# Top-k attention with a highway feed-forward layer on one core: joined remainder groups, fewer check operations, another order at the start and at the end

## The chip, the cores and the metric

The kernel runs on one core of a Trainium2 chip. The metric is the device time of one execution in microseconds (us). The kernel before was timed three times: 926.5, 925.96 and 923.73, median 925.96. The profile is of one more execution, of 925.72.

## The reference

Eight batches of eight heads, 576 rows, head dimension 64. For each row of scores only the 32 largest count, the softmax is taken over these, and the result, laid side by side for the eight heads, goes through a highway layer of width 512.

```python
scores = scale * np.matmul(q, k.transpose(0, 1, 3, 2))
kth = np.partition(scores, -top_k, axis=-1)[..., -top_k:-top_k + 1]
scores = np.where(scores >= kth, scores, -1000000000.0)
attn = softmax(scores);  x = attn @ v, heads side by side
H = np.maximum(x @ w_h, 0.0);  T = sigmoid(x @ w_t + b_t)
out = T * H + (1.0 - T) * x
```

## The kernel before

**Tiles and steps.** A batch has 576 = 4 x 128 + 64 rows, hence five groups: four of 128 rows and a remainder of 64. A full group has eight tiles (one a head), handled two at a time as "pairs", four pairs; in a remainder group two heads share a tile of 128 partitions, so there are four tiles and two pairs. That makes 18 pairs a batch and 144 in all, in 40 groups. The main loop has one step n for each pair and some more to drain. In step n, work on several pairs is interleaved: the score matmuls of pair n+1 (`scores`, into a four-bank tile `ps` of which there is one) and their evacuation by ScalarE into z (`evac`); the first reduction of pair n on VectorE (`tree`, the operation hi<-ps,z); for two pairs together the next two halvings (`folds`) and the minima that belong to them, on GpSimd (POOL; `minima`, with integer arithmetic); the first half of the top-k lists of two pairs (`tops`), in even steps, and the rest (`rest`) in odd steps, all MAX8 and MATCH_REPLACE8 on VectorE, which leaves the 32nd largest in m4; the penalty of pair n-4 (`mask`, ScalarE); transposes of scores and penalty with an exponential on the way out (`trans`); the product with v of pair n-5 (`av`) and its copy to xs.

**End of a group.** `norm` takes the reciprocal of the sums (VectorE) and multiplies (POOL) to x. The feed-forward layer follows in three pieces, one a step, from a list: `ffn_x` (transposes xtps, copies xT and xh on ScalarE), `ffn_h` and `ffn_d` (matmuls hps on TensorE, then d on VectorE), `ffn_t`, `ffn_e` and `ffn_o` (matmuls tps, tanh on ScalarE, d again on VectorE, o on POOL, store by SyncE). All of xtps, hps, tps and kqps use the pool `fps`, which has one bank: the next cannot begin until the last is read.

**Loads.** For each pair of heads `prep_pair` loads k, q and v (four loads each: two heads, main part and end), transposes k and q on TensorE into kqps and copies them out on ScalarE. The first batch does it in the first four steps, ahead of `tree`; later batches spread it. All loads and stores but a few are issued by SyncE (SP) in one queue. The weights are loaded from POOL's queue in step 1.

**Checks.** After each group `settle` (POOL, three operations: room, slack, reach) records how far the lists reached; at the end VectorE reduces these records, TensorE transposes the result, and a flag says whether a second, exact body has to run. It is read by all engines into a register, and a branch follows.

**What sets the order.** All instructions of TensorE, VectorE, ScalarE and POOL in the main body are recorded in program order (`Pinned`, L35, so that nearly all rows carry this line). SyncE's order is chosen by the scheduler.

The order of a step in the kernel before, and its drain:

```python
while step < NPR + 6 or ffn:
    ...
    if have(n):
        ops.tree(n)
    ...
    if have(n - 4):
        ops.mask(n - 4, *pairs[n - 4], tis=(0,))
    ...
    if have(n - 5):
        ops.av(n - 5, g, pi, preps[g.b][2])
    if have(n - 4):
        ops.mask(n - 4, *pairs[n - 4], tis=(1,))
```

Of the kernel before, what the change touches and what calls it, by code (L numbers as in the profile page):

```python
# [18 lines left out]
WIDE = 600.0  # L19
J = 4  # L20
# [26 lines left out]
class Group:  # L47


    def __init__(self, b, qt, gi, H, P):  # L50
        self.b, self.qt, self.gi = b, qt, gi
        self.rem = qt == J
        self.qlen = P // 2 if self.rem else P
        tiles = (
            [(2 * hp, 2 * hp + 1) for hp in range(H // 2)]
            if self.rem
            else [(h,) for h in range(H)]
        )
        self.nt = len(tiles)
        self.pairs = [tiles[i : i + 2] for i in range(0, self.nt, 2)]  # L60


class Ops:
# [31 lines left out]
    def load_pair(self, src, hp, name, eng=None):  # L95
        nc, D, S, R, P = self.nc, self.D, self.S, self.R, self.P
        JP = J * P
        t = self.ldpool.tile([P, J + 1, 2, D], FP32, tag=name, name=name)
        eng = eng or nc.sync
        for hh in range(2):  # L100
            h = 2 * hp + hh
            eng.dma_start(
                t[:, 0:J, hh, :], src(h, 0, JP).rearrange("(p j) d -> p j d", j=J)
            )
            eng.dma_start(t[0:R, J, hh, :], src(h, JP, S))
        return t
# [6 lines left out]
    def prep_pair(self, srcs, hp, prep, qeng=None):  # L113

        nc, D, S, R, P = self.nc, self.D, self.S, self.R, self.P
        JP = J * P
        kT, qT, vb = prep
        ins = {}

        def load():  # L120
            ins["k"] = self.load_pair(srcs[1], hp, "kin")
            ins["q"] = self.load_pair(srcs[0], hp, "qin", qeng)
            ins["v"] = self.load_pair(srcs[2], hp, "vin")

        def main(name, dst):
            kqps = self.fps.tile([P, 512], FP32, tag="fp", name="kqps")
            for c in range(J):
                nc.tensor.transpose(
                    kqps[:, c * P : (c + 1) * P],
                    ins[name][:, c, :, :].rearrange("p h d -> p (h d)"),  # L130
                    self.ident[:],
                )
            nc.scalar.copy(dst[:, hp, 0:JP], kqps[:])

        def last():
            kqps = self.fps.tile([P, 512], FP32, tag="fp", name="kqps")
            for i, name in enumerate("kq"):
                nc.tensor.transpose(
                    kqps[:, i * R : (i + 1) * R],
                    ins[name][0:R, J, :, :].rearrange("p h d -> p (h d)"),  # L140
                    self.ident[0:R, 0:R],
                )
            for i, dst in enumerate((kT, qT)):
                nc.scalar.copy(dst[:, hp, JP:S], kqps[:, i * R : (i + 1) * R])

        def values():
            vdst = vb[:, 2 * hp : 2 * hp + 2, :, 0:D].rearrange("p h c d -> p c h d")
            nc.scalar.copy(vdst[:, 0:J], ins["v"][:, 0:J])
            nc.scalar.copy(vdst[0:R, J], ins["v"][0:R, J])

        return [load, lambda: main("k", kT), lambda: main("q", qT), last, values]


# [47 lines left out]
    def folds(self, k, g, pi):  # L201
# [4 lines left out]
        if pi == 0:  # L206
            g.w2 = self.lpool.tile([P, H, H2 + 24], FP32, tag="w2", name="w2")
# [29 lines left out]
    def tops(self, g, t, h3, hl):  # L237
# [5 lines left out]
        m1, m2, w2 = g.m1[:, t, :], g.m2[:, t, :], g.w2[:, t, :]  # L243
# [13 lines left out]
    def rest(self, g, t, lo):  # L257
# [6 lines left out]
        w2 = g.w2[:, t, :]  # L264
# [29 lines left out]
    def lists(self, n, g, pi):  # L294
        P, H = self.P, self.H
        if pi == 0:
            for name in ("m1", "m4") if self.exact else ("m1", "m2", "m4"):
# [20 lines left out]
    def settle(self, g):  # L318
# [7 lines left out]
            self.room[:, g.gi, 0:nt, 0:3],  # L326
            thr.unsqueeze(2).to_broadcast([P, nt, 3]),
# [3 lines left out]
        gp.tensor_tensor(  # L331
            self.slack[:, g.gi, 0:nt, 0], g.m2[:, 0:nt, 7], thr, ALU.subtract
        )
        gp.tensor_copy(self.reach[:, g.gi, 0:nt], g.m1[:, 0:nt, 0])
# [44 lines left out]
    def trans(self, n):  # L379
# [4 lines left out]
        zr = self.zrps.tile([P, 512], FP32, tag="zr", name="zr")  # L384
        for ti in range(2):
            self.chunk_T(zr[:, ti * P : (ti + 1) * P], z, pen, ti, J)
        nc.scalar.activation(
            et[:, :, J, :],
            zr[:, 0 : 2 * P].rearrange("p (t j) -> p t j", t=2),
            AF.Exp,  # L390
            scale=self.scale,
        )
# [10 lines left out]
        self.st[n].update(et=et, zr=zr)  # L403

    def av(self, n, g, pi, vb):
# [4 lines left out]
        if pi == 0:  # L410
            g.xs = self.xpool.tile([P, self.H * DE], FP32, tag="xs", name="xs")
        ql = g.qlen
        c0 = col = 0 if g.rem else 2 * P
        h0 = g.pairs[pi][0][0]
        for ti, heads in enumerate(g.pairs[pi]):
            for hi, h in enumerate(heads):
                q0 = hi * (P // 2)
                for c in range(J + 1):
                    nc.tensor.matmul(
                        zr[0:ql, col : col + DE],  # L420
# [6 lines left out]
        nc.scalar.copy(g.xs[0:ql, h0 * DE : h0 * DE + col - c0], zr[0:ql, c0:col])  # L427
# [3 lines left out]
    def norm(self, g):  # L431
        nc, P, H, D = self.nc, self.P, self.H, self.D
        ql = g.qlen
        xs3 = g.xs[0:ql, :].rearrange("p (h e) -> p h e", e=D + 1)
        rinv = self.xpool.tile([P, H], FP32, tag="rinv", name="rinv")
        nc.vector.reciprocal(rinv[0:ql, :], xs3[:, :, D])
        g.x = self.xpool.tile([P, H * D], FP32, tag="x", name="x")
        nc.gpsimd.tensor_tensor(
# [6 lines left out]
    def ffn_x(self, g):  # L445
        nc, P, n_g, ql = self.nc, self.P, self.n_g, g.qlen
# [16 lines left out]
    def ffn_h(self, g):  # L463
        nc, P, n_g, ql = self.nc, self.P, self.n_g, g.qlen
# [10 lines left out]
    def ffn_d(self, g):  # L475

        ql = g.qlen
# [10 lines left out]
    def ffn_t(self, g):  # L488

        nc, P, n_g, ql = self.nc, self.P, self.n_g, g.qlen  # L490
        g.ps = self.fps.tile([P, 512], FP32, tag="fp", name="tps")
# [13 lines left out]
    def ffn_e(self, g):  # L505

        ql = g.qlen
# [9 lines left out]
    def ffn_o(self, g, dst):  # L517
        ql = g.qlen
        o = self.fpool.tile([self.P, self.dm], FP32, tag="o", name="o")
        self.nc.gpsimd.tensor_tensor(o[0:ql, :], g.x[0:ql, :], g.d[0:ql, :], ALU.add)  # L520
        self.nc.sync.dma_start(dst, o[0:ql, :])
# [3 lines left out]
def kernel(  # L525
# [17 lines left out]
    assert D == 64 and R == 64 and H % 4 == 0 and dm == 512  # L543
# [13 lines left out]
    nc.vector.tensor_scalar_mul(nident[:], ident[:], -STEEP)  # L557
# [11 lines left out]
    for i in range(2):  # L569
# [5 lines left out]
    room = const([P, NG, H, 3], FP32, "room")  # L575
    nc.gpsimd.memset(room[:], 1.0)
    slack = const([P, NG, H, 1], FP32, "slack")
    nc.gpsimd.memset(slack[:], 1.0)
    reach = const([P, NG, H], FP32, "reach")
    nc.gpsimd.memset(reach[:], 1.0)  # L580
# [8 lines left out]
        room=room, slack=slack, reach=reach,  # L589
    )  # L590

    with ExitStack() as cm:
# [12 lines left out]
        def srcs(b):  # L605
            return [
                (lambda h, r0, r1, t=t: t[b, h, r0:r1, :]) for t in (q, k, v)
            ]

        def out_rows(g):  # L610
            if not g.rem:
                r0 = g.b * S + g.qt
                return out[r0 : r0 + JP : J, :]
            r0 = g.b * S + JP
            return out[r0 : r0 + R, :]

        groups = [
            Group(b, qt, b * nck + qt, H, P) for b in range(B) for qt in range(nck)
        ]
        pairs = [(g, pi) for g in groups for pi in range(len(g.pairs))]  # L620
# [6 lines left out]
        def prep(b, hp, qeng=None):  # L627
            if hp == 0:
                preps[b] = ops.prep_alloc(vbufs[b % 2])
            return ops.prep_pair(srcs(b), hp, preps[b], qeng)  # L630
# [20 lines left out]
        early = [prep(0, hp, nc.scalar if hp == 0 else None) for hp in range(NHP)]  # L651
# [8 lines left out]
        step = 0  # L660
        late = []
        while step < NPR + 6 or ffn:
            n = step
            if n + 1 < NHP:
                for piece in early[n + 1][1:4]:
                    piece()
                if n + 2 < NHP:
                    early[n + 2][0]()
            if have(n):
                ops.tree(n)  # L670
                if n % 2:
                    ops.minima(n // 2, ops.folds(n // 2, *pairs[n - 1]))
            if n == 1:
# [3 lines left out]
            post = None  # L677
            if ffn:
                pre, post = ffn.pop(0)
                pre()  # L680
# [3 lines left out]
            if have(n - 4):  # L684
# [7 lines left out]
            ended = have(n - 5) and pairs[n - 5][1] == len(pairs[n - 5][0].pairs) - 1  # L692
# [8 lines left out]
            else:  # L701
# [3 lines left out]
                if post:  # L705
                    post()
                if ended:
                    ops.norm(pairs[n - 5][0])
                ops.run(gens)
            if have(n - 4):  # L710
# [7 lines left out]
            if ended:  # L718
# [6 lines left out]
                        lambda g=g: (ops.ffn_e(g), ops.ffn_o(g, out_rows(g))),  # L725
# [3 lines left out]


        ok = const([P, 4], FP32, "ok")
        vec = nc.vector
        vec.tensor_reduce(ok[:, 0:1], room[:], op=ALU.min, axis=AX.XYZ)
        vec.tensor_reduce(ok[:, 1:2], slack[:], op=ALU.min, axis=AX.XYZ)
        vec.tensor_reduce(ok[:, 2:3], reach[:], op=ALU.max, axis=AX.XY)
        bad = const([P, 4], FP32, "bad")
        vec.tensor_scalar(bad[:, 0:1], ok[:, 0:1], TINY, None, ALU.is_lt)
        vec.tensor_scalar(bad[:, 1:2], ok[:, 1:2], 0.0, None, ALU.is_lt)
        vec.tensor_scalar(bad[:, 2:3], ok[:, 2:3], WIDE, None, ALU.is_gt)
        vec.tensor_reduce(bad[:, 3:4], bad[:, 0:3], op=ALU.max, axis=AX.X)  # L740
        bps = ops.fps.tile([P, 512], FP32, tag="fp", name="bps")
        nc.tensor.transpose(bps[0:1, 0:P], bad[:, 3:4], ident[:])
        flag_f = const([1, 1], FP32, "flag_f")
        vec.tensor_reduce(flag_f[:], bps[0:1, 0:P], op=ALU.max, axis=AX.X)
        flag = const([1, 1], I32, "flag")
        vec.tensor_copy(flag[:], flag_f[:])

    taken = nc.values_load(flag[0:1, 0:1], min_val=0, max_val=1)
    with tc.If(taken > 0):
        with tc.For_i(0, B, 1) as b:  # L750
            with ExitStack() as cm:
                ops = Ops(cm, tc, shared, exact=True)
                srcs = [
                    (lambda h, r0, r1, t=t: t[bass.ds(b, 1), h, r0:r1, :].rearrange("o s d -> (o s) d"))
# [58 lines left out]
```

## Time and profile before

| what | us |
|---|---|
| median of three executions | 925.96 |
| the profiled execution | 925.72 |
| its span, first to last instruction | 923.9 |
| VectorE (DVE) busy | 873.4 |
| TensorE (PE) busy | 730.8 |
| GpSimd (POOL) busy | 709.5 |
| ScalarE (ACT) busy | 699.2 |
| SyncE's loads and stores, share of the 16 DMA engines | 16.6% |

How to read the lines that follow. A row of the timeline gives start and duration in us, engine, line of the code, operation, target and sources, shape, the number of instructions merged, and in brackets the engine's idle time before it and what ended that. A row of the groups gives, after the shape and the count, busy us, the mean duration in ns, and idle us before with what ended most of it. A row of waits gives who waited for whom, us in total, times, and the longest. PEld is TensorE's weight load, SPq the queue of SyncE. The mean granted TensorE clock was 0.944 of full speed; in single stretches of about 3.4 us it was 0.5.

### The profile page before, as it was taken

What the parts mean: (1) busy time and instruction counts of PE and PEld (TensorE: products, weight loads), DVE (VectorE), ACT (ScalarE), POOL (GpSimd) and SP (SyncE); (2) the same over time, 40 slices, a digit from 0 to 9 for tenths busy, and PEclk for the clock granted to TensorE, in tenths of its full rate; (3) what the DMA queues carried; (4) which work ended last, traced back from release to release, by engine and by line L of the source; (5) the groups of instructions that cost most, each with busy time, mean ns of one, the idle gap of its engine ahead of it and who ended that gap; (6) DMA issues with size and microseconds to landing.
All of it is one profiled execution on the core that took longest, in us unless ns stands there. A gap on an engine that the chain in (4) does not pass through costs nothing.

```text
span 923.9 us, 20386 instructions
## 1 busy us (share of the span) xinstructions
PE 730.8 (79%) x6601; PEld 510.6 (55%) x6601; DVE 873.4 (95%) x4234; ACT 699.2 (76%) x1321; POOL 709.5 (77%) x509
## 2 busy tenths in 40 slices
PE   5687878878788887878888787887879878877774
PEld 3355556555565555555655555655646555555552
DVE  4699999999999999999999999999999999999991
ACT  3488778887787886887878886888868878776772
POOL 3777778877877888777788887887787778877761
PEclk9999899999999998998999999999989989998997
DMA  5731220221103220122202212023100300000000
GB/s 114 138 70 40 51 51 13 58 69 45 38 18 69 61 52 12 46 51 51 51 13 56 50 41 51 13 67 73 46 24 25 71 12 13 12 13 7 13 24 21
DMA packets 123298, 40.33 MB, mean 44 GB/s; under 512 B 117424, under 2 KB 118576, under 8 KB 123184
## 3 DMA queue, kind: packets, MB, share of 16 engines
q1 hardware_dynamic: 120768, 37.48, 16.6%
q0 software_dynamic: 1200, 1.18, 0.8%
q8 instruction: 54, 0.88, 0.4%
q14 instruction: 60, 0.49, 0.2%
q10 hardware_dynamic: 1216, 0.30, 0.1%
HBM read 30.67 MB, written 9.44 MB: 43 GB/s over the span
## 4 chain that ended last, share of the span: by engine, by line
DVE 78%; POOL 8%; PE 7%; ACT 3%; issue 2%; SPq 1%; DMA 1%; POOLq 0%; ACTq 0%; DVEq 0%
DVE w L35 37%; DVE m L35 18%; DVE hi L35 9%; DVE hh L35 6%; DVE d L35 5%; POOL hi L35 4%; DVE h L35 3%; PE ps L35 2%; POOL hh L35 2%; PE zt L35 2%; POOL o L35 1%; PE zr L35 1%; PE xtps L35 1%; POOL x L35 1%; PE kqps L35 1%
## 5 line engine op out<-in xcount | busy, mean ns | idle before, releaser
L35 PE MATMUL ps<-kT,qT 64*128 64x64 f32 (+3 forms) x1280 | 221.9, 473 | 48.8 <-DVE hi L35 47.8
L35 ACT ACTIVATE z<-ps 128x1152 f32<-128x1152 f32 x144 | 163.0, 1132 | 96.7 <-PE ps L35 95.6
L35 POOL TENSOR_TENSOR hh<-hi,hh 128x576 int32<-128x576 int32 x72 | 101.6, 1410 | 171.9 <-DVE w L35 171.7
L35 PE MATMUL zt<-ident,z 128*128 128x128 f32 x1152 | 225.1, 289 | 0.0
L35 ACT ACTIVATE pen<-z,m 128x576 bf16<-128x576 f32 x288 | 224.1, 779 | 0.2 <-DVE m L35 0.2
L35 PE MATMUL zt<-nident,pen 128*128 128x128 bf16 x1152 | 214.5, 226 | 0.0
L35 DVE MAX8 m<-w 128x8 f32<-128x168 f32 (+1 forms) x864 | 203.6, 283 | 0.0
L35 PEld LDWEIGHTS ps<-kT,qT 64*128 64x128 f32 (+1 forms) x1280 | 112.8, 191 | 148.2 <-issue 88.5
L35 POOL TENSOR_TENSOR hi<-hi,z 128x1152 int32<-128x1152 int32 x72 | 190.1, 2641 | 5.6
L35 POOL TENSOR_TENSOR hi<-z,hi 128x1152 int32<-128x1152 int32 x72 | 189.3, 2629 | 5.6
L35 PEld LDWEIGHTS zt<-ident,z 128*128 128x128 f32 x1152 | 169.8, 147 | 18.4
L35 ACT ACTIVATE et<-zt 128x512 bf16<-128x512 f32 x288 | 161.9, 602 | 15.5 <-PE zt L35 14.1
L35 PEld LDWEIGHTS <-pen 128*128 128x128 bf16 x1440 | 161.0, 112 | 6.3 <-ACT pen L35 6.3
L35 DVE MATCH_REPLACE8 w<-m,w 128x72 f32<-128x72 f32 (+1 forms) x576 | 148.3, 265 | 0.0
L35 DVE TENSOR_TENSOR hi<-ps,z 128x576 f32<-128x576 f32 x144 | 106.3, 738 | 21.6 <-ACT z L35 21.5
L35 DVE MAX8 w<-hi 128x8 f32<-128x288 f32 x288 | 116.5, 445 | 0.0
L35 POOL TENSOR_TENSOR hh<-hh,hi 128x576 int32<-128x576 int32 x72 | 101.4, 1408 | 5.6
L35 PEld LDWEIGHTS <-et 128*128 128x128 bf16 (+1 forms) x1600 | 70.4, 104 | 36.3 <-ACT et L35 13.8
L35 PE MATMUL zr<-v,et 128*128 128x65 bf16 (+1 forms) x1600 | 82.4, 199 | 5.1 <-ACT et L35 4.9
L35 DVE MAX8 w<-hh 128x8 f32<-128x72 f32 x576 | 83.9, 216 | 0.0
L35 PE MATMUL zr<-ident,z 128*128 128x128 f32 x288 | 76.8, 320 | 3.9 <-ACT xs L35 3.9
L35 PE MATMUL xtps<-ident,x 128*128 128x128 f32 (+1 forms) x160 | 28.0, 304 | 60.4 <-POOL x L35 51.1
(64 smaller groups left out, 1102.7 us busy)
## 6 DMA issues: line engine op xcount, KB each, us to landing
kin<-in_k_dram SPq DMA_DIRECT2D x64, 128.0 KB, 2.7
vin<-in_v_dram SPq DMA_DIRECT2D x64, 128.0 KB, 2.6
out_dram<-o SPq DMA_DIRECT2D x32, 256.0 KB, 2.3
qin<-in_q_dram SPq DMA_DIRECT2D x62, 128.0 KB, 2.6
kin<-in_k_dram SPq DMA_DIRECT2D x64, 16.0 KB, 2.5
vin<-in_v_dram SPq DMA_DIRECT2D x64, 16.0 KB, 2.3
out_dram<-o SPq DMA_DIRECT2D x8, 128.0 KB, 2.3
qin<-in_q_dram SPq DMA_DIRECT2D x62, 16.0 KB, 2.4
```

The source lines that it names most:

```text
L35: return self._tc.keep_in_program_order(fn(*args, **kw))
```

## The change

- **Joint remainders.** The remainder groups of two successive batches share one tile xs of 128 rows (rows 0 to 63 and 64 to 127) and go through normalisation and feed-forward once; the result is stored by two stores of 64 rows.
- **Checks.** The second list m2 lies in the row of w2, beside the other lists, so `settle` is one POOL operation (room, four wide) instead of three; the third check looks at the reciprocals, which are kept in a tile `scales`. The reductions stand in step NPR+4 (`judge_lists` after group 38's first d, `judge_scales` after the last normalisation), the flag is made ahead of the last second d.
- **First batch.** k and q are transposed into the two banks of `ztps`, only the ends into `fps`; q is copied out by VectorE; the copies of a step come after `tree`, not ahead of it. The first k and q loads are split over SyncE and ScalarE. k, q: three loads a pair instead of four; v: two, with a row order that moves four rows in one piece. The scaled identity nident is made by ScalarE. The weights are loaded in step 5.
- **End.** In the last steps both masks of the last pair come first, then `av`, then `trans` with its end part last, then the feed-forward piece. The last group multiplies x and sums o on VectorE, and its tps uses a bank of `ztps`.

SyncE's queue in the built program then has the reading of the flag ahead of the last two stores; before, it was behind the last store. Core of the diff:

```diff
+            if early:
+                kqps = self.ztps.tile([P, 512], FP32, tag="zt", name="kqps")
+            else:
+                kqps = self.fps.tile([P, 512], FP32, tag="fp", name="kqps")
...
-            nc.scalar.copy(dst[:, hp, 0:JP], kqps[:])
+            if early and name == "q":
+                nc.vector.tensor_copy(dst[:, hp, 0:JP], kqps[:])
+            else:
+                nc.scalar.copy(dst[:, hp, 0:JP], kqps[:])
...
-        m1, m2, w2 = g.m1[:, t, :], g.m2[:, t, :], g.w2[:, t, :]
+        m1, w2 = g.m1[:, t, :], g.w2[:, t, :]
+        m2 = w2[:, H2 + 24 : H2 + 32]
...
-        gp.tensor_tensor(
-            self.slack[:, g.gi, 0:nt, 0], g.m2[:, 0:nt, 7], thr, ALU.subtract
-        )
-        gp.tensor_copy(self.reach[:, g.gi, 0:nt], g.m1[:, 0:nt, 0])
...
-        nc.gpsimd.tensor_tensor(
+        (nc.vector if g.final else nc.gpsimd).tensor_tensor(
             g.x[0:ql, :].rearrange("p (h d) -> p h d", h=H),
...
+        if g.final:
+            g.ps = self.ztps.tile([P, 512], FP32, tag="zt", name="tps")
+        else:
+            g.ps = self.fps.tile([P, 512], FP32, tag="fp", name="tps")
...
-    nc.vector.tensor_scalar_mul(nident[:], ident[:], -STEEP)
+    nc.scalar.mul(nident[:], ident[:], -STEEP)
...
+        def judge_lists():
+            vec.tensor_reduce(ok[:, 0:1], room[:, :, :, 0:3], op=ALU.min, axis=AX.XYZ)
+            vec.tensor_reduce(ok[:, 1:2], room[:, :, :, 3:4], op=ALU.max, axis=AX.XYZ)
+            vec.tensor_scalar(bad[:, 0:1], ok[:, 0:1], TINY, None, ALU.is_lt)
+            vec.tensor_scalar(bad[:, 1:2], ok[:, 1:2], 0.0, None, ALU.is_gt)
...
+            final = n >= NPR + 3
+            if final and have(n - 4):
+                ops.mask(n - 4, *pairs[n - 4], tis=(1,))
...
-            ended = have(n - 5) and pairs[n - 5][1] == len(pairs[n - 5][0].pairs) - 1
+            ended = False
+            if have(n - 5):
+                g, pi = pairs[n - 5]
+                ended = pi == len(g.pairs) - 1 and (not g.rem or g.r0 > 0)
...
                     post()
+                if n == NPR + 4:
+                    judge_lists()
                 if ended:
                     ops.norm(pairs[n - 5][0])
+                if n == NPR + 4:
+                    judge_scales()
```

## The prediction

> **What bounds the kernel now.** I read the page first: which engine is full, and in which slices of the span it is not.
>
> ```profile
> PE 730.8 (79%) x6601; PEld 510.6 (55%) x6601; DVE 873.4 (95%) x4234; ACT 699.2 (76%) x1321; POOL 709.5 (77%) x509
> DVE  4699999999999999999999999999999999999991
> ```
>
> VectorE is the bound, at nine tenths or more in 37 of 40 slices; only the two slices at the start and the one at the end have room. So an edit between them pays what it takes off VectorE's queue, and edits at the ends pay what they take off the chains that feed and drain it. Next the waits of VectorE, asked for three stretches, 0 to 46.2, 46.2 to 875 and 875 to the end (us in total, times, longest):
>
> ```profile
> DVE hi L35 <- ACT z L35: 18.3, 4, 6.1
> ...
> DVE hi L35 <- ACT z L35: 3.3, 5, 1.1
> DVE d L35 <- PE hps L35: 2.0, 3, 0.7
> ...
> DVE d L35 <- PE hps L35: 6.4, 2, 4.2
> DVE d L35 <- ACT tps L35: 4.3, 2, 3.0
> ```
>
> In the middle 828.8 us hold 5.3 us of waits. At the head VectorE waits for the evacuated scores of the first four steps, at the tail for the last two groups' feed-forward chain. The timeline of the head shows why:
>
> ```profile
> 1.57 7.00 DVE L557 TENSOR_SCALAR nident<-ident 128x128 bf16<-128x128 f32 x1 [1.57 <-POOL ident masks.py:199]
> 8.13 0.36 POOL L580 MEMSET reach<- 128x320 f32 x1
> 13.01 0.76 DVE L35 TENSOR_TENSOR hi<-ps,z 128x576 f32<-128x576 f32 x1 [4.43 <-ACT z L35]
> 14.21 1.12 PE L35 MATMUL kqps<-ident,qin 128*128 128x128 f32 x4 [1.37 <-ACT kT L35]
> 16.27 2.34 PE L35 MATMUL ps<-kT,qT 64*128 64x512 f32 x7
> 19.83 0.76 DVE L35 TENSOR_TENSOR hi<-ps,z 128x576 f32<-128x576 f32 x1 [6.06 <-ACT z L35]
> 34.54 0.76 DVE L35 TENSOR_TENSOR hi<-ps,z 128x576 f32<-128x576 f32 x1 [3.36 <-ACT z L35]
> ```
>
> The score reductions ("hi", one a step) start at 13.01, 19.83, 26.64 and 34.54; after 34.54 VectorE doesn't wait again for long. In each step TensorE transposes k into the one bank of this pool, waits until ScalarE has copied it out, transposes q, waits again, transposes the two ends, and only then multiplies. Behind that, SyncE issues 12 loads for a head pair, one each 0.65 us, which is 7.9 us, and the fourth step is paced by this.
>
> **The head.** I lay the new order on the durations above. First k: its two heads now leave from two queues at 0.76 (before, the second left at 2.40 and landed 3.2 us later), so the k transposes can start at 4.0 (3.6 to 4.6), q's at 5.1, for they have a bank of their own and the second pair of loads leaves at 1.45. VectorE copies q at 6.25. That copy is not in the trace: the nearest rows are ScalarE's copy of the same tile (0.58) and VectorE's 128x512 operations from PSUM (0.68, next start after 0.60); I take 0.65. Scores 6.95 to 9.3, evacuation 1.13, first reduction 10.5 instead of 13.01.
>
> Then the period, from the end E of one step's scores: k and q transposes 2.2, copy of q until E+2.9; beside it ScalarE does the evacuation (until E+1.2), the values (0.81), k's copy and the two ends, until E+2.95; scores 2.35. That is 5.3 to 5.4 instead of 6.8 to 7.9. Third reduction near 21.3, end of the third step's copy of q 22.9. In VectorE's queue this copy stands ahead of the first lists, 27.32 to 31.18 before, 3.86 us; they end at 26.8, and the fourth reduction, whose scores are ready at 26.5, runs then: 26.8 against 34.54, and VectorE has done the same list work by then. Loads: 8 for a pair at 0.65 us are 5.2 us, so SyncE just keeps up; the fourth pair's last q load is the 27th, issued at 17.8, landed by 20.5 at the 2.6 us of before, wanted at 21. **Head: -7.7 us.** Bounds: -8.8 (first k at 3.6, the copies at 0.58) and -4.8 (below).
>
> Here a row and a rule differ. The row: nident, 128 elements a partition, took 7.00 us and ended when POOL's memsets did (8.49). By it the first q copy at 6.25 would be held until 8.5, and the head would give 2 us less. The Trainium skill (SBUF — State Buffer, Who interferes with whom) says that VectorE and GpSimd exclude each other only where VectorE uses a two-port mode or has two SBUF inputs, and that an operation with at most one SBUF input outside these modes isn't touched; a source in PSUM gives no two-port mode (VectorE: DVE Perf Modes). By it the copy isn't held. I take the rule, since a third row agrees with it: the reduction from PSUM and z at 26.64 took its usual 0.76 while POOL worked from 25.27 to 27.89. nident itself goes to ScalarE, between its table load (at 2.1 instead of 3.45, two issues being gone) and the first k copy at 5.1: free; and if it weren't, some 0.3 us.
>
> The weights' loads go behind four more pairs of POOL operations, to about 39 us; wanted at step 10, about 66, landed 6.2 to 10 us after issue. They cost POOL 2.26 us once, between two runs of minima: 8.1 us of the 11.3 to 12 us of two steps are used. Nothing.
>
> **The middle.** Eight groups of 64 rows become four of 128. VectorE loses, four times:
>
> ```profile
> L35 DVE SCALAR_TENSOR_TENSOR d<-tps,d 64x512 f32<-64x512 f32 x8 | 5.4, 674 | 3.1 <-ACT tps L35 3.0
> L35 DVE SCALAR_TENSOR_TENSOR d<-hps,xh 64x512 f32<-64x512 f32 x8 | 5.3, 665 | 2.2 <-PE hps L35 2.2
> L35 DVE RECIPROCAL rinv<-xs 64x8 f32<-64x8 f32 x8 | 1.5, 184 | 0.4 <-ACT xs L35 0.4
> ```
>
> Durations overlap, so I take the distance to the next start: 0.60, 0.60 and 0.11 (889.76 to 890.36, 895.05 to 895.64, 878.91 to 879.02). 4 x 1.31 = 5.2 us. By durations it would be 6.1. A row of 128 instead of 64 partitions costs VectorE the same (672 to 681 ns in full groups). POOL loses 4 x (1.27 + 1.04) and two of three check operations in each group (20 us), ScalarE and TensorE four groups' share; none of that is on the path. It could ease the 23 of 70 folds that take 0.89 to 0.94 us instead of 0.76, but these lie beside the normalisation of full groups, which stay. The second list now lies in the row of w2: the same instructions with the same waits. **Middle: -5.2 us**, from -4.4 (the waits grow by 0.8) to -6.1.
>
> **The tail.**
>
> ```profile
> 905.98 0.69 DVE L35 SCALAR_TENSOR_TENSOR d<-hps,xh 128x512 f32<-128x512 f32 x1 [4.24 <-PE hps L35]
> 907.07 0.20 DVE L35 RECIPROCAL rinv<-xs 64x8 f32<-64x8 f32 x1 [0.40 <-ACT xs L35]
> 909.45 0.43 PE L35 MATMUL xtps<-ident,x 64*128 64x64 f32 x4 [1.49 <-DVE d L35]
> 912.25 1.86 PE L35 MATMUL tps<-wt,xT 128*64 128x512 bf16 x4 [0.84 <-DVE d L35]
> 915.99 1.25 POOL L35 TENSOR_TENSOR o<-x,d 64x512 f32<-64x512 f32 x1 [5.29 <-issue]
> 917.27 0.50 SPq L521 DMA_DIRECT2D out_dram<-o  x1
> ```
>
> On the old time axis: both last masks run at 900.66 to 902.1 (the second ended at 903.35), so the last values' product ends at 904.8, not 906.6. But group 38's hps stands behind it now, so d still comes at 905.8. Behind d stand, new on this path, the check reductions (1.15 and 0.48, and two small ones: 1.6 us); they sat in an idle gap at 899.43 before. Then reciprocal and x on VectorE (0.7, POOL took 1.03) until 908.9, the check of scales (0.6), and group 38's second d until 910.15; it frees the bank for the last transposes: 910.25, 0.8 later than before, and xtps and xT of 128 rows cost 0.4 more. hps starts at 911.55, 1.2 late. From there it gains: tps has another bank and follows at 912.45 without the wait (it started at 912.25), and o is on VectorE (0.65 for 1.25 and a change of engine). o ends at 916.0 if TensorE has full clock, at 916.8 if tps runs at the granted 0.5 that it had from 912.3 on (1.86 us for what took 1.02 at 906.72); before: 917.24. SyncE reads the flag before the last two stores instead of after them, so its 1.5 us from 917.8 to 919.3 is hidden, and one more store issue (0.4) comes. After the branch some 4.5 us follow as before (SP 919.3, end 923.9; but TensorE's own branch took 3.8). **Tail: -1.3 us**, from +0.5 to -2.9.
>
> **Sum.** 923.9 - 7.7 - 5.2 - 1.3 = 909.7 span. The profiled execution took 925.72, 1.8 more than its span, 0.24 under the median of 925.96: 911.5.
>
> **Rivals.**
> - *The loads pace the head.* For: the DMA engines were 0.74 busy from 23.1 to 46.2 at 138 GB/s, and the load rate rises by a third; k and q keep their 256-byte pieces. Against: v now goes in pieces of 1,024 bytes, and the weights leave this stretch. With a period of 6.4 the fourth reduction comes at 10.5 + 19.2 = 29.7: head -4.8, time 914.4.
> - *The middle doesn't close up.* The removed operations would become waits for z or hps. Against: 5.3 us of waits in 828.8 us. Head and tail alone: 916.7.
> - *Slower.* One mechanism: the second list as needles and target in one tile could cost VectorE the overlap of successive operations. Four MAX8 of 0.21 take 0.63 in the trace, so the overlap is some 0.06 each, about 0.14 for a MAX8 and its MATCH_REPLACE: 288 x 0.14 = 40 us, 951. It decides from 14.4 / 288 = 0.05 us a list on. Against: the list lies apart from what the same operation writes, all waits are the same, and MAX8 already writes into w2 at its usual 216 ns.
> - *The tail gives back more*: checks on the path and a slow TensorE clock, +0.5: 913.3, inside the range.
>
> **Chances.** Forecast 0.62 (907 to 914), loads 0.17, middle 0.11, tail 0.07, slower 0.03. A measurement of this kernel can tell 0.3% (2.8 us) from no change: faster 0.96, within it 0.01, slower 0.03. The range leaves out the slower case and the outer ends: 907 to 917.
>
> **What would show it.** "hi" starts near 10.5, 16, 21 and 27, its wait for z in the head under 11 us; the first q copy at 0.6 to 0.7 us (at 2 or more the rule was wrong). d and reciprocal x36 on VectorE, and equal time between like steps otherwise. MAX8 and MATCH_REPLACE means unchanged within 3 ns. xtps of the last group later than before relative to the last list, the last store earlier. I am wrong if the fourth "hi" stays past 30, or if VectorE's waits in the middle pass 8 us.

## The result, and the profile after

| | us |
|---|---|
| changed kernel, median of four executions (909.42 to 913.79) | 912.18 |
| kernel before on the same chip, median of four | 925.85 |
| ratio, with its 95% interval | 0.9853 (0.982 to 0.9887) |
| the profiled execution, and its span | 913.79, 912.0 |

The change takes off 1.5%. The sum named 909.7 for the span and 911.5 for the time; the profiled execution has 912.0 and 913.79. Of its three terms only the first came out as written.

On the page of the changed kernel, the engines' totals and VectorE's slices:

```profile
PE 727.2 (80%) x6549; PEld 508.7 (56%) x6549; DVE 865.3 (95%) x4227; ACT 692.4 (76%) x1306; POOL 683.8 (75%) x419
...
DVE  2999999999999999999999999999999999999973
```

VectorE is still the bound in 37 slices, with 8.1 us less work, but they are now the second to the 38th instead of the third to the 39th: the head is shorter, and the drain begins earlier and is no shorter. VectorE's waits, in the stretches 0 to 38, 38 to 878 and 878 to the end (us in total, times, longest):

```profile
DVE qT L35 <- PE kqps L35: 8.5, 3, 6.8
DVE hi L35 <- ACT z L35: 8.3, 3, 3.7
...
DVE hi L35 <- ACT z L35: 2.7, 4, 1.1
DVE d L35 <- PE hps L35: 0.8, 2, 0.6
...
DVE d L35 <- PE hps L35: 11.6, 2, 7.8
```

The wait for z in the head is 8.3 us instead of 18.3; of the 8.5 for qT, 6.8 are the start of the program. The middle has 3.5 us of waits instead of 5.3. In the tail the wait for hps grew from 6.4 to 11.6, and the 4.3 for tps are gone. The timeline of the head:

```profile
3.42 0.31 ACT L604 ACTIVATE nident<-ident 128x128 bf16<-128x128 f32 x1
...
6.79 0.69 DVE L35 COPY qT<-kqps 128x512 f32<-128x512 f32 x1 [6.79 <-PE kqps L35]
...
6.98 0.90 POOL L623 MEMSET room<- 128x960 f32 x1
...
11.23 0.76 DVE L35 TENSOR_TENSOR hi<-ps,z 128x576 f32<-128x576 f32 x1 [3.74 <-ACT z L35]
...
15.22 0.76 DVE L35 TENSOR_TENSOR hi<-ps,z 128x576 f32<-128x576 f32 x1 [2.64 <-ACT z L35]
...
15.97 0.63 PE L35 MATMUL kqps<-ident,qin 128*128 128x128 f32 x4 [1.25 <-DMA qin<-in_q_dram]
...
20.80 0.76 DVE L35 TENSOR_TENSOR hi<-ps,z 128x576 f32<-128x576 f32 x1 [1.95 <-ACT z L35]
...
27.03 0.76 DVE L35 TENSOR_TENSOR hi<-ps,z 128x576 f32<-128x576 f32 x1
```

The four reductions stand at 11.2, 15.2, 20.8 and 27.0, where 10.5, 16, 21.3 and 26.8 were forecast, and the fourth waits for no other engine: it stands behind VectorE's own lists. The first copy of q took 0.69 us while POOL's memset ran beside it. In steps three and four TensorE waited for a load of q (1.25 us here, and 0.82 before the transposes at 21.47), so the loads now only just keep up. The groups of the feed-forward show the four groups gone:

```profile
L35 DVE SCALAR_TENSOR_TENSOR d<-hps,xh 128x512 f32<-128x512 f32 x36 | 24.7, 687 | 12.4 <-PE hps L35 12.4
...
L35 DVE SCALAR_TENSOR_TENSOR d<-tps,d 128x512 f32<-128x512 f32 x36 | 24.4, 677 | 0.0
...
L35 DVE RECIPROCAL scales<-xs 128x8 f32<-128x8 f32 x36 | 7.2, 201 | 0.4 <-ACT xs L35 0.4
```

And the timeline of the tail, where the last list starts at 882.72:

```profile
888.92 0.61 PE L35 MATMUL xtps<-ident,x 128*128 128x128 f32 x4
...
890.49 1.04 PE L35 MATMUL hps<-wh,xT 128*128 128x512 bf16 x4
...
891.64 0.69 DVE L35 SCALAR_TENSOR_TENSOR d<-hps,xh 128x512 f32<-128x512 f32 x1 [7.77 <-PE hps L35]
892.25 1.77 DVE L35 TENSOR_REDUCE ok<-room 128x1 f32<-128x960 f32 x2
...
895.73 0.68 DVE L35 SCALAR_TENSOR_TENSOR d<-tps,d 128x512 f32<-128x512 f32 x1
896.47 1.12 PE L35 MATMUL xtps<-ident,x 128*128 128x128 f32 x4 [2.84 <-DVE d L35]
...
898.27 1.89 PE L35 MATMUL hps<-wh,xT 128*128 128x512 bf16 x4 [0.69 <-ACT xT L35]
899.95 1.91 PE L35 MATMUL tps<-wt,xT 128*128 128x512 bf16 x4
...
903.51 0.69 DVE L35 TENSOR_TENSOR o<-x,d 128x512 f32<-128x512 f32 x1
904.23 2.27 SPq L568 DMA_DIRECT2D out_dram<-o  x2
```

Two things are to be seen. The reductions hold VectorE for 1.77 us between group 38's first d and the last x. And TensorE is at half clock in the whole last chain, from xtps to tps: for group 38, a few us earlier, xtps took 0.61 and hps 1.04 us (the first two rows), and for the last group they take 1.12 and 1.89.

To compare runs I cut each profiled span into five: up to the start of the fourth "hi"; from there to the start of the last list (the last MAX8 from w); to the start of group 38's first d; to the end of the last sum o; and the rest. The last three together are called the tail. All from the timelines, in us:

| kernel (profiled execution) | 4th hi | to last list | to first d | to end of o | rest |
|---|---|---|---|---|---|
| before | 34.5 | 862.9 | 8.6 | 11.3 | 6.7 |
| changed | 27.0 | 855.7 | 8.9 | 12.6 | 7.8 |
| changed, once more (control) | 26.4 | 856.2 | 8.6 | 12.5 | 6.9 |
| remainders apart | 26.3 | 862.9 | 8.2 | 11.4 | 5.8 |
| one bank | 32.0 | 855.6 | 7.2 | 12.6 | 7.9 |
| lists judged early | 26.6 | 853.9 | 7.0 | 10.3 | 7.2 |
| old order at the end | 26.6 | 852.9 | 9.4 | 12.1 | 7.4 |
| judged early, old order | 26.6 | 852.3 | 9.4 | 9.0 | 7.0 |
| judged early, last store on ScalarE | 26.9 | 857.2 | 8.9 | 11.3 | 6.5 |
| nident on VectorE | 26.5 | 854.5 | 9.0 | 12.7 | 7.0 |
| 19 filler products | 26.7 | 854.9 | 8.4 | 13.0 | 7.0 |
| 8 filler products | 26.5 | 851.4 | 7.0 | 10.4 | 7.6 |
| one store for both | 26.7 | 854.9 | 9.1 | 12.7 | 10.5 |
| judged early, old order, one store | 27.0 | 853.8 | 8.8 | 9.1 | 10.7 |

By the first two rows the change gave 7.5 in the head and 7.2 in the middle, and took 2.8 in the tail (0.4, 1.3 and 1.1). By the control it gave 8.1 and 6.7 and took 1.6. The two agree in the signs, and differ by 0.5 to 1.2 us in the single terms.

### The profile page after: what moved, and what is told of

The parts are those of the page before. It is cut to its first block, busy times and chain, and to the rows that moved or that the text cites. A ratio compares the mean times of both kernels' runs of the same rounds, so it can differ in the third digit from the quotient of the medians.

```text
span 912.0 us, 19916 instructions
## 1 busy us (share of the span) xinstructions
PE 727.2 (80%) x6549; PEld 508.7 (56%) x6549; DVE 865.3 (95%) x4227; ACT 692.4 (76%) x1306; POOL 683.8 (75%) x419
## 3 DMA queue, kind: packets, MB, share of 16 engines
q0 software_dynamic: 1200, 1.18, 0.9%
## 4 chain that ended last, share of the span: by engine, by line
DVE 81%; POOL 8%; PE 6%; ACT 2%; issue 1%; DMA 1%; SPq 0%; POOLq 0%; ACTq 0%; DVEq 0%
DVE w L35 42%; DVE m L35 16%; DVE hi L35 9%; DVE hh L35 6%; DVE d L35 4%; POOL hi L35 4%; DVE h L35 3%; POOL hh L35 2%; PE ps L35 2%; PE zt L35 1%; POOL o L35 1%; PE xtps L35 1%; PE zr L35 1%; POOL x L35 1%; DMA qin<-in_q_dram 1%
## 5 line engine op out<-in xcount | busy, mean ns | idle before, releaser
L35 PE MATMUL ps<-kT,qT 64*128 64x64 f32 (+3 forms) x1280 | 226.5, 481 | 58.2 <-DVE hi L35 55.1
L35 DVE MAX8 m<-w 128x8 f32<-128x168 f32 x576 | 161.1, 323 | 0.0
L35 DVE TENSOR_TENSOR hi<-ps,z 128x576 f32<-128x576 f32 x144 | 107.9, 749 | 11.2 <-ACT z L35 11.0
L35 DVE MATCH_REPLACE8 w<-m,w 128x168 f32<-128x168 f32 x288 | 89.7, 321 | 0.0
L35 PE MATMUL xtps<-ident,x 128*128 128x128 f32 x144 | 27.1, 318 | 54.0 <-POOL x L35 44.4
```

The source lines that it names most:

```text
L35: return self._tc.keep_in_program_order(fn(*args, **kw))
```

## The experiments

Times are medians of 4 to 6 executions. The kernel before ran beside each set: 925.64 beside the remainders apart, one bank, lists judged early and the old order alone; 924.61 beside the control, the old order with early judging, the store on ScalarE and nident; 924.15 beside 19 fillers and the two with one store; 924.36 beside 8 fillers. All edits are to the changed kernel. That kernel again, as a control:

> The changed kernel itself, as a control on the same chip and in the same rounds as the next three. All theories: within 1.5 us of 912.2.

Measured: 912.67 (912.21 to 913.99), ratio 0.9875 (0.9859 to 0.9891). It repeats within 0.5 us.

**Remainders apart.**

```diff
-            Group(b, qt, b * nck + qt, H, P, joint=True)
+            Group(b, qt, b * nck + qt, H, P, joint=False)
```

with one store of 64 rows for each remainder again.

> The changed kernel with the remainder groups apart again, all else as changed. Theory (each of the four groups costs VectorE 1.3 us of its own queue and nothing else): the stretch from the fourth first reduction to the last MAX8 grows from 855.7 to about 860.9 us, the time by 5 us to about 917. Rival 1 (the whole 7.2 us by which this stretch shrank belong to the joining, by waits of the 64-row groups too): 863 us in the stretch, time about 919. Rival 2 (the removed operations had been cover for waits): under 2 us of difference, time under 914.

Measured: 916.21 (915.18 to 917.13), ratio 0.9904 (0.9888 to 0.992). By the time the joint groups are worth 3.5 to 4.0 us, between the 5 of the theory and the 2 of its second rival; by the stretches they are worth more in the middle and give some back at the end. From the fourth "hi" to the last list it has 862.9, and its waits there are 4.6 us:

```profile
DVE hi L35 <- ACT z L35: 3.3, 5, 1.1
DVE d L35 <- PE hps L35: 1.3, 2, 0.7
```

Without waits that is 858.3, and 857.6 in the kernel before; the joint ones have 852.2 (changed, 855.7 - 3.5), 852.7 (control, 3.5 of waits) and 851.4 (eight fillers, none). So VectorE's queue is 5.6 to 6.9 us shorter for the joint groups, and they do close up. The tail of the kernel with the remainders apart is 3.8 us shorter than the changed kernel's and 2.6 shorter than the control's: its last group has 64 rows and one store. It also met the half clock for 3.4 us ahead of the end of o and not for 6.8, and how much of the difference that is was not separated.

**One bank.**

```diff
-            prep(0, hp, nc.scalar if hp == 0 else None, True) for hp in range(NHP)
+            prep(0, hp, nc.scalar if hp == 0 else None, False) for hp in range(NHP)
```

> The changed kernel with the first batch's k and q transposed through the one bank and both copied by ScalarE, but with the new loads and queues. Theory (bank and copying engine set the period of the head): transposes of q wait for k's copy again, period near 6.8 us, first reductions near 11.7, 18.5, 25.3 and 32.0 instead of 11.23, 15.22, 20.80 and 27.03, time about 5 us longer, 917. Rival (the loads set it, since 12 became 8 and two queues start): the fourth reduction stays under 29, time under 914.

Measured: 919.49 (917.12 to 920.63), ratio 0.9941 (0.9925 to 0.9958). Its head:

```profile
25.22 0.76 DVE L35 TENSOR_TENSOR hi<-ps,z 128x576 f32<-128x576 f32 x1 [4.41 <-ACT z L35]
...
26.42 1.12 PE L35 MATMUL kqps<-ident,qin 128*128 128x128 f32 x4 [1.37 <-ACT kT L35]
...
32.04 0.76 DVE L35 TENSOR_TENSOR hi<-ps,z 128x576 f32<-128x576 f32 x1 [2.28 <-ACT z L35]
```

TensorE waits 1.37 us for ScalarE's copy of k, as before the change, and the steps are 6.82 us apart. Banks and VectorE's copy are worth 32.04 - 27.03 = 5.0 us of the head. The other 2.5 are what the rest of the change does there, mostly the new loads: k's first transposes start at 4.20 here and at 5.63 before the change, and the fourth step takes 6.8 us instead of 7.9. By the medians this kernel is 6.8 to 7.3 us slower, more than its head shows; the profiled execution is the fastest of its six, and where the others lost more is not known.

**Lists judged early.** The reductions over room stand one step earlier, in a stretch where VectorE waits for hps anyhow (7.8 us in the changed kernel):

```diff
                 ops.run(late, 2)
+                if n == NPR + 3:
+                    judge_lists()
...
-                if n == NPR + 4:
-                    judge_lists()
```

> The changed kernel with the check of the lists one step earlier, in the gap of VectorE before group 38's first d. Theory (these reductions, 1.9 us, stand on the path from that d to the last group's x and to group 38's second d): the second d comes when tanh ends, 1.4 us earlier, and the end with it: tail after the last MAX8's start 27.9 instead of 29.3, time about 910.8. Rival (the tail is long for TensorE's half clock and the branch, not for the checks): the tail changes by less than 0.5 us.

Measured: 908.8 (906.5 to 910.51), ratio 0.9825 (0.9806 to 0.9845); 3.4 to 3.9 us less than the changed kernel. The tail:

```profile
887.46 0.69 DVE L35 SCALAR_TENSOR_TENSOR d<-hps,xh 128x512 f32<-128x512 f32 x1 [3.00 <-PE hps L35]
888.07 0.19 DVE L35 RECIPROCAL scales<-xs 128x8 f32<-128x8 f32 x1
...
890.10 0.69 DVE L35 SCALAR_TENSOR_TENSOR d<-tps,d 128x512 f32<-128x512 f32 x1 [0.33 <-ACT tps L35]
...
890.85 0.66 PE L35 MATMUL xtps<-ident,x 128*128 128x128 f32 x4 [1.40 <-DVE d L35]
...
892.19 1.40 PE L35 MATMUL hps<-wh,xT 128*128 128x512 bf16 x4 [0.69 <-ACT xT L35]
```

From the first to the second d it takes 2.64 us instead of 4.09: 1.45, the size expected. Its profile gained 4.7 us in the tail. Of the rest, 1.9 lie before the first d and 0.6 behind o, and 0.8 in the last chain, where TensorE's half clock began at hps and not at xtps. So the edit is shown to be worth about 1.5 us; the median's further 2 us cannot be put down to it.

**Old order at the end**, alone and with the lists judged early:

```diff
-            final = n >= NPR + 3
+            final = False
```

> The changed kernel with the old order of masks, transposes and feed-forward piece in the last steps; x and o of the last group stay on VectorE, the checks stay where the change put them. Theory (behind the checks the reordering buys nothing: group 38's hps moved behind the last values' product, d came 8.92 us after the last MAX8's start instead of 8.55): time equal or up to 0.5 us shorter, d at 8.5 to 8.6. Rival (the reordering is worth the 1.3 to 1.8 us by which the last product comes earlier): time 1.5 us longer.

Measured: 910.12 (908.0 to 914.1), ratio 0.985 (0.9826 to 0.9875). The first d came at 9.4 after the last list and not at 8.5 to 8.6, in an execution with 6.8 us of half clock shortly ahead (see the last section).

> The lists judged early, and the old order of masks, transposes and feed-forward piece in the last steps. Theory (with the checks off the path the last group's normalisation follows the last product, which the new order brings earlier): 1 us slower than with the lists judged early alone, 2.4 us under the control. Rival (the new order puts group 38's hps behind that product and gains nothing): as fast or up to 1 us faster.

Measured: 907.08 (906.02 to 908.16), ratio 0.9814 (0.98 to 0.9827): below the changed kernel (the control beside it had 0.9859 to 0.9891). No gain from the new order of the last steps is to be seen; with it the time is 1.7 to 2.6 us longer, an edge that the spread of single executions does not let me call certain. In the profile of the second the whole last chain ran at full clock (xtps 0.66, hps 1.04, tps 1.03).

**The last store on ScalarE**, with the lists judged early:

```diff
-            self.nc.sync.dma_start(dst, o[i * n : (i + 1) * n, :])
+            q = self.nc.scalar if g.final and i else self.nc.sync
+            q.dma_start(dst, o[i * n : (i + 1) * n, :])
```

> The lists judged early as in the third run, and of the last group's two stores the second issued by ScalarE instead of SyncE. Theory (in the changed kernel the second store's issue took 1.70 us on SyncE, and SyncE's branch and its 3.0 us behind it wait for that): the end comes 1.5 us earlier than with the lists judged early alone, 5 us under the control. Rival (the time behind the last sum is set by the fetch after the branch, whoever issues): no difference to the third run, 3.4 us under the control.

Measured: 909.47 (907.07 to 912.52), ratio 0.9828 (0.9812 to 0.9844), against 908.8 without it: no gain. Both stores now leave at 904.33 in 0.5 us each, and the rest after o is 6.5 us instead of 7.2, but no time comes of it that the spread would show. The 1.5 us of the theory are not there.

**nident on VectorE.**

```diff
-    nc.scalar.mul(nident[:], ident[:], -STEEP)
+    nc.vector.tensor_scalar_mul(nident[:], ident[:], -STEEP)
```

> The changed kernel with nident made by VectorE again. Theory (SBUF to SBUF with a constant, so a two-port mode that POOL's memsets exclude until they end near 8.7): nident ends at 8.6 to 8.8, the first q copy behind it in VectorE's queue starts then instead of at 6.79, the fourth first reduction comes at 28.5 to 29 instead of 27.03, time 1.8 us over the control. Rival (the 7 us were nident's own time, or cost nothing): the q copy is not delayed, time within 0.5 us of the control.

Measured: 913.75 (911.55 to 914.41), ratio 0.9885 (0.987 to 0.99). Its head:

```profile
1.57 6.39 DVE L604 TENSOR_SCALAR nident<-ident 128x128 bf16<-128x128 f32 x1 [1.57 <-POOL ident masks.py:199]
...
6.73 1.23 DVE L35 COPY qT<-kqps 128x512 f32<-128x512 f32 x1
...
8.41 0.42 POOL L626 MEMSET scales<- 128x320 f32 x1
...
11.73 0.76 DVE L35 TENSOR_TENSOR hi<-ps,z 128x576 f32<-128x576 f32 x1 [3.76 <-ACT z L35]
```

nident takes 6.39 us again (on ScalarE it took 0.31), and the first copy of q ends 0.5 us later. But it ends at 7.96, not at the 8.6 to 8.8 of the theory, while POOL's last memset runs on to 8.83: it was not held until the memsets were over, and what sets its 6.39 us stays open. The first "hi" is 0.5 later and the fourth, at 26.54, not later at all. The loss is real in the row and absorbed within three steps. The median is 1.1 us above the control's, with intervals that overlap.

**Filler products.** To test the half clock I put products of constants, which nobody reads, into TensorE's queue in the drain:

```diff
+                for _ in range({4: 4, 5: 12, 6: 3}.get(n - NPR, 0)):
+                    spare = ops.bigps.tile([P, 2, 1024], FP32, tag="big", name="spare")
+                    ops.nc.tensor.matmul(spare[:, 0, 0:512], nident[:], wh[:, 0, :])
```

> The changed kernel with 19 products of constants (128x512 bf16, into the free score banks, read by nobody) in TensorE's queue: 4 after group 38's hps, 12 after its tps, 3 after the last group's xtps. Theory (the half clock in the last chain comes from TensorE's idle stretches between these, 0.85 and 2.84 us in the trace, and it costs there what the rows say): xtps 1.12 becomes 0.61, hps 1.89 becomes 1.04, tps 1.91 becomes 1.02, of which 0.5 + 0.85 and the part of tps that isn't covered lie on the path: the end comes 1.9 us sooner, about 910.6 where the changed kernel has 912.5. Rival (the low clock is left over from earlier work, or the end is set elsewhere): durations as in the changed kernel or time within 0.6 us of it.

Measured: 912.5 (911.15 to 913.92), ratio 0.9875 (0.9857 to 0.9892): no gain, and yet the clock did what the theory says:

```profile
892.37 5.13 PE L35 MATMUL spare<-wh,nident 128*128 128x512 bf16 x12
...
897.34 0.60 PE L35 MATMUL xtps<-ident,x 128*128 128x128 f32 x4
...
898.85 1.02 PE L35 MATMUL hps<-wh,xT 128*128 128x512 bf16 x4
899.72 1.03 PE L35 MATMUL tps<-wt,xT 128*128 128x512 bf16 x4
```

The clock stays up and the chain from xtps to the end of o takes 5.69 us instead of 7.73. But a product took 0.43 us (5.13 / 12), and the 12 held TensorE until 897.3, 2.5 us past the end of the second d (894.83) that xtps waits for. With fewer (`{4: 1, 5: 6, 6: 1}`):

> The changed kernel with 8 products of constants (1 after group 38's hps, 6 after its tps, 1 after the last group's xtps) instead of the 19. A product took 0.43 us there, so that the 12 after tps held TensorE for 5.13 us and the last transposes, free to start about 895.5, began at 897.34. Theory (only this overrun ate what the full clock gave, 5.69 us from the last transposes to the end of the last sum instead of 7.73): 6 take 2.6 us and end before the transposes are due; the end of the last sum comes 2.0 us sooner after the last list (+19.4 to +19.7 instead of +21.2 to +21.5), time about 910.4. Rival (six are not enough, the clock falls to half again): xtps 1.1, hps and tps 1.9, time 912.5.

Measured: 907.19 (904.52 to 909.18), ratio 0.9819 (0.9801 to 0.9837).

```profile
886.71 2.54 PE L35 MATMUL spare<-wh,nident 128*128 128x512 bf16 x6
...
889.72 0.66 PE L35 MATMUL xtps<-ident,x 128*128 128x128 f32 x4 [0.47 <-DVE d L35]
...
891.06 1.04 PE L35 MATMUL hps<-wh,xT 128*128 128x512 bf16 x4 [0.47 <-ACT xT L35]
891.94 1.03 PE L35 MATMUL tps<-wt,xT 128*128 128x512 bf16 x4
```

From the first d to the end of o there are 10.4 us instead of 12.6: the 2.2 that the half clock cost. The median is 5.0 to 5.5 us lower, more than that. The rest lies ahead of the fillers (1.9 us before the first d, 4.3 in the middle of the profiled execution), so the profile does not give it to them; whether it was only this set of executions stays open. What the fillers are shown to be worth is 2.2 us.

**One store for a joint group**, alone and with the two best edits:

```diff
-            ends = [(g.b + i) * S for i in (0, 1)]
-            return [out[r1 - R : r1, :] for r1 in ends]
+            both = out.rearrange("(c i s) n -> c i s n", i=2, s=S)
+            return [both[g.b // 2, :, JP:S, :]]
```

> The changed kernel with one store of 2 x 64 rows for a joint group instead of two. Theory (the second issue, 1.70 us on SyncE at the end, is on the path behind the last sum): from the end of the last sum to the end of the span 7.8 and 6.9 us become 5.8 to 6.2, as with the single store of 64 rows (5.82): about 911.2. Rival (what follows the last sum is set by the branch and not by the stores): 6.7 or more remain, time as the changed kernel's 912.5.

Measured: 914.75 (912.88 to 919.27), ratio 0.99 (0.9878 to 0.9922).

> List checks early, the old order of the last steps, and one store for a joint group. Theory (as for the single store alone; the parts add): 907.08 - 1.0 = 906.1. Rival: 907.1, nothing from the store.

Measured: 910.8 (910.53 to 912.95), ratio 0.9859 (0.9842 to 0.9877). Both theory and rival fell: it is slower by 2.1 to 2.6 and by 3.7 us. After the end of o (903.36) the DMA engines of the first of these two kernels, in two stretches (the last two columns are their mean busy share and GB/s):

```profile
903.40:907.00 3.60, 0.00 (x0) 0.00 (x0) 0.00 (x0) 0.00 (x0) 0.00 (x0) 0.68 0.15 38
907.00:912.00 5.00, 0.00 (x0) 0.00 (x0) 0.00 (x0) 0.00 (x0) 0.00 (x0) 0.50 0.11 42
```

and of the changed kernel after its own (904.20):

```profile
904.20:908.00 3.80, 0.00 (x0) 0.00 (x0) 0.00 (x0) 0.00 (x0) 0.00 (x0) 0.64 0.36 84
908.00:912.00 4.00, 0.00 (x0) 0.00 (x0) 0.00 (x0) 0.00 (x0) 0.00 (x0) 0.50 0.02 6
```

A busy share of 0.11 to 0.15 of 16 engines is about two engines. The 256 KB trickle out at about 40 GB/s until shortly before 912, where two stores are done by 908, and the program's end waits for them: SyncE's branch came sooner, at 904.1 instead of 906.6, but its last wait behind the branch ended at 912.1 instead of 910.2. The Trainium skill (DMA: Bandwidth & Descriptors, Why a DMA increments its semaphore by 16 and not by 1) says that a transfer is spread over the largest number of engines, up to 16, that divides the slowest dimension of both its sides; with two batches outermost that is 2. The rows agree.

## Why the prediction was right, and where it was wrong

**The head was right** (-7.5 for -7.7), in its mechanism too. The first "hi" came 0.7 us later than forecast and the fourth 0.2. The banks make the difference that they were said to make, the fourth "hi" is held by VectorE's own queue, and the loads just keep up (the two waits for q say how narrowly). The rule taken over the row was the right one: with POOL's memset beside it the copy of q took 0.69 us and not the 2 us or more that nident's 7.00 suggested. nident on ScalarE was free as forecast: it ends at 3.73, and k's first copy starts at 5.41. (That nident's 7.00 us ended with POOL's memsets need not mean that they held it: moved back to VectorE, it ended 0.9 us before them.)

**The middle was larger** (-7.2 for -5.2, outside its bounds of -4.4 to -6.1). The queue became shorter by 5 to 6 us (857.6 to 851.4 up to 852.7 without waits): the distance to the next start, which I took for the operations, gave 5.2, their durations would have given 6.1. The other part is 1.8 us less waiting for z and hps, and that is luck of the execution as far as can be seen: in the profiles of kernels with the same middle these waits were anything from 0.0 to 4.7.

**The tail has the wrong sign** (+2.8 for -1.3; the control +1.6); it is the term that failed. Its pieces do not add up to -1.3 even as written: o 1.2 us sooner, the flag's 1.5 us hidden and 0.4 for one more store make -2.3, or -1.5 with the slow tps, and the text does not say what stands against that. Laid side by side, from the last list: first d forecast at 8.4, measured 8.9; xtps at 12.8, measured 13.75; end of o at 18.6 (19.4 with a slow tps), measured 21.5; the rest 6.7 - 1.5 + 0.4 = 5.6, measured 7.8. So

- 0.5 before the first d;
- 0.4 between it and xtps: the checks are 1.77 and 0.27 us where 1.6 were counted. The cost was seen, and its remedy not: early judging takes 1.45 us off this piece;
- 2.0 from xtps to the end of o, the half clock. I had let it touch tps alone, as in the trace of before, and not xtps and hps; the fillers show its price, 2.0 and 2.2 us;
- 2.2 after o. The second store's issue was costed at 0.4 and took 1.70 (0.93 in the control), and from SyncE's branch to the end it took 5.4 us where 4.5 were counted. Reading the flag ahead of the stores did help: in the kernel with the remainders apart, which does that with one store, the rest is 5.8 instead of 6.7. The control, with 6.9 instead of 7.8, says that this term is also partly chance.

That is 5.1 in all, the difference between -2.3 and +2.8; against the -1.3 that went into the sum it is 4.1. In the sum, the error of the middle (2.0 too little gain) and of the tail (4.1 too much) cancelled to 2.3 us, so that 912.18 came so near to 911.5 is in part luck.

**The rivals.** Loads pacing the head: no, though nearly. The middle not closing up: no, the kernel with the remainders apart shows it. The slower one, the lists in one tile: the mean records of MAX8 and MATCH_REPLACE are 3 to 15 ns longer in the changed kernel, so the sign "within 3 ns" failed as worded. But a row of eight MAX8 over 72 values mostly lasts 1.18 us instead of 1.16 or 1.17, and one of four 0.62 or 0.63 instead of 0.61 or 0.62. The kernel with the remainders apart, which has the new lists, needs 858.3 us without waits against 857.6 before: by this the queue lost 0.7 us. The tail giving back more: yes, and more than its +0.5.

## What to carry to other kernels

The end of a pipelined kernel has to be costed by the clock it will have there: here the last chain, behind a stretch in which TensorE worked little, ran at half clock and took 2.0 to 2.2 us more. A few filler products, counted to end before the next step is due, may be a cheap cure. Checks and other side work belong in the wait that is longest, not in the gap that is nearest to their operands. And before stores are joined, see which dimension is outermost.

## What the runs showed of the hardware

**The half clock near the end.** In the changed kernel TensorE worked 1.24 of the 3.41 us before 895.01 (the first number after the stretch's length), and the granted clock (the column behind the engines) was 0.50 for the 6.83 us after it, in which lies nearly all of TensorE's part of the last chain. With eight fillers it worked 2.66 and 2.48 us in such stretches, and the clock stayed at 1.00. Of the changed kernel:

```profile
866.72:874.72 8.00, 6.34 (x38) 4.49 (x39) 7.93 (x36) 4.39 (x9) 6.24 (x4) 0.57 0.09 34
891.60:895.01 3.41, 1.24 (x5) 0.38 (x4) 3.34 (x8) 0.58 (x1) 0.00 (x0) 1.00 0.00 0
895.01:901.84 6.83, 4.69 (x13) 2.03 (x14) 2.02 (x6) 1.12 (x2) 1.26 (x1) 0.50 0.10 38
```

Of the one with eight fillers:

```profile
861.90:869.90 8.00, 5.13 (x56) 3.89 (x57) 7.93 (x35) 5.63 (x12) 6.29 (x5) 1.00 0.09 34
886.92:890.33 3.41, 2.66 (x11) 0.87 (x9) 2.64 (x9) 0.57 (x1) 0.54 (x1) 1.00 0.00 0
890.33:893.75 3.42, 2.48 (x12) 0.88 (x10) 1.08 (x3) 1.65 (x3) 0.73 (x1) 1.00 0.20 77
```

The clock fell 1.4 us after TensorE's last product, halfway through its gap of 2.84. The Trainium skill (TensorE: Matmul & The Clock Gate, Part 1: The HAM clock gate) gives an idle window of about 3.4 us as what halves the clock; here a window with 1.24 us of work in it was enough. All fourteen traces say the same, read from 35 us on: the clock changes only at instants of a grid, 3.413 us apart, whose place differs from trace to trace. Each of the 331 falls from 1.0 to 0.5 follows a grid stretch in which TensorE's rows have at most 1.93 us of work, and of the stretches at full clock with less than 1.54 us all but one were followed by 0.5. Between these two figures it went either way. Each of the 322 rises follows a half-clock stretch with at least 3.06 us of work.

**A low clock ahead of the drain goes with a later drain.** The first lines of the two fences are the stretch from 16 to 8 us before the last list. In runs without a low clock there, the first d came 7.0 to 7.2 us after the last list; in those with 3.4 us of it 8.2 to 8.8, in those with 6.8 us 8.9 to 9.4, over all fourteen profiled executions, kernel before included. No run sets the clock there on purpose, so the cause is read from this order and not tested. The low clock falls in one place or another from run to run (the changed kernel had 6.8 us of it there and its control 3.4), and may be part of the 2 to 6 us by which executions of one kernel differ; single edits of the tail can't be read finer than that from one profile.

**A strided reduction** of 320 values (the fourth column of room) took 0.71 us where one of 320 values in a row took 0.48.
